# First pair's forward stage and the weight preparation put into the hand-given order, a shorter routing, and a newly searched order

## The chip, the core and the metric

The kernel runs on one core of a Trainium2 chip. The core has five engines with one instruction queue each: TensorE (PE, matmuls; PEld is its weight loading), VectorE (DVE), ScalarE (ACT), GpSimd (POOL) and SyncE (SP, which here only issues transfers). An engine takes its instructions strictly in the order of its queue, so one that waits holds all behind it. Transfers run on 16 DMA engines that all queues share. The metric is the device time of one execution in microseconds (us); lower is better.

## What is computed

The reference is two layers. For x of 8 batches x 1856 rows x 256 columns:

```python
X = rfft(x, axis=1)                       # 929 complex rows per batch
Yr = shrink(Xr @ w_r - Xi @ w_i + b_r)    # shrink(v) = sign(v) * max(|v| - 0.01, 0)
Yi = shrink(Xr @ w_i + Xi @ w_r + b_i)
x  = irfft(Yr + 1j * Yi, n=1856).reshape(14848, 256)
g  = argmax(x @ w_group)                  # 4 groups, then 4 experts of the group
e  = argmax(x @ w_expert[g])
out = softmax weight of g * softmax weight of e * (relu(x @ w1[g, e]) @ w2[g, e])
```

Each of the 14848 rows (tokens) goes through one of 16 experts (256 to 1024 to 256).

## The kernel before, in words

The 8 batches are worked as 4 pairs. For each pair the kernel runs these stages, each a function whose calls are "steps" named by one letter:

- `c` (`a_mm`, 8 per pair): first-stage DFT matmuls of x (L327) into a PSUM bank; `d` (`a_turn`, 16 per pair): VectorE transposes of the bank (L331). There are three such banks (`pa`, `bufs=3`), shared by many steps.
- `e f h i g` (`f_mm` L599 and copies and subtractions that split the result in a high and a low part), then `j y z k m o` (spectral matmuls L642 and L657 against the prepared weights, bias, shrink).
- `r s` (`b_mm` L682, `b_turn` L690), `v w x` (`p_mm` L701, `p_out` L713 with a store to `ys_d` in DRAM, `p_turn` L723): inverse transform.
- `G H` (gate logits), `R` (`route_steps`: one instruction of `route_g` each, 33 per half pair, 264 in all): which expert a token goes to and which slot of that expert's list. `S` (`scatter`, 128 in all): one indirect transfer each, issued by GpSimd, that writes 128 tokens' (row, weight) entries into the lists `lst` in DRAM (L242). From the 65th on at most five are on their way at once.
- Early expert work on the first rows of four experts' lists, 8 jobs: `I` loads a piece of the lists (L779), `Z` turns it into indices on GpSimd, `F` gathers the rows from `ys_d` (L427, GpSimd), `T X Y` transpose and split them (L804), `U A B` multiply by w1 (L825, 12 matmuls a step), `D E J` multiply by w2 (L849 and L851 in turn, 4 of each a step), `K` stores (L507, GpSimd). `W V` split the weights, `l` loads x and weights (SP).
- `L` loads all lists (L882, L886), `M` gathers the first rows of the main loop (`gi_h`).

The string `ORDER` lists the letters. Each letter runs the next step of its kind, and within it TensorE, VectorE, ScalarE, SP and GpSimd keep that order exactly; nothing is moved at run time. Behind `ORDER` comes the main expert loop over all 16 experts, which is fixed.

Two parts stand ahead of the order in the version before: the first pair's first stage (8 x `lead_mm`, each with two `turn_a`), and the preparation of the spectral weights (`wh`, `wl`, `wsum`, `bias`: L363 to L370). There the build's own scheduler sets the order. In `ORDER` of before, `c` and `d` stand for pairs 1 to 3 alone (24 and 48), and two loads (`CI`, `wg`) are held behind the first pair's last transpose (`a_last`).

Of the kernel before, what the change touches and what calls it, by code (L numbers as in the profile page):

```python
# [36 lines left out]
ORDER = """  # L37
jcddjcdedffehhiicggfhyzfydzkimdhokiejmggfocjfhyyzdkzihkmigogjmeffcoyhdjziykhzkedgigcmmojdefyfodhjyhizizkggdmkcoemjfoyjhz
ykifdmdzkghicmogjoyjffdyzkhmhizkidgmoeegjyfofzhjyihkizmggokjmfeyozhkfijhieggmoyfjfyhzzhikiggmkmffojrosjyshhyiirlzkmggssz
rksorsmojsyscejzdffdcdhihyllkgzigdmvcwcxxlwvdodjdkdxwyxzvcmwwcxkdddxvdwcxmwxcwdddooGdvHRexwjRRfwvxRRjfhywRxRzRhRvxiRigww  # L40
kRgmRRxReRxvRowwRxyRfjRhRzRReyiikRwxRRRzgkmRgfRRomoRfjjRlRhhGyiyHRzfRRRgkRSzmkhRRRRSigomRojefjeRyyRlRzhkzfRiRRShRRSSSRRS
SmgRioRgjRkfymRRhiiRzkSggeofmjoRRSSjhRfhyfihiyrgSzgksrzmkRsmssSrSoosjjeyszfhfyrhkizkmgssiSRvomgjoxcdwjwvxdxRSyyzRwzwvxwe
xffSxvkxwShwhwxikmmGoSSiojSjvgSwRSgHRxRRxRRvcwxRydywRdxvRRwcxlzSzRRwwdRvxSRkRRxkRdewmRxwfcoRfRhjRiGShgRSmddSRoiHcRgeyfRd
SjdfhiRzRRhyzRRSklikgmeSgRmoSRfocRRjSjRchfRSdigySRdzRRydSkmzdkeRRhciRSSoSmlRjSgodjRyfzRRRhfydSkRRSRlzRShmReiikojRggRfSyR
mRRRfeRhzRhiSoRikjgSgRymojrzfhSfiyhiszgkSRkgmmsRroojjRyRszSysrsszkmrWSosSSefkjSsvfmhShigSigxWowvwSyxxSvvwwxVxjezwwyfSkwx
fxmzhxhiSSRokmVSwogWiVjWGgvvHvRyxRwjxxRwRvRRRwxSRxRzRwRweSxwfyzRhRRkRxfRwxmkwRhiReRRmgRioRRGfgRjoRSRIhWRRRWWZyjyzRRiiRzk
keggSSHRmfohmojRRfSyjhRzyfRihkRzSRgiRRmRgkmoSRejfoyfRjzhyRSzRRhSSiiSSRgVkSgmRkSojRRyRRmRzSRRkVRRRomSVorRRRRsFWTsRFRXYVSr
sSUsrlURVslsABABrSSSsSSWUAsVUBWvvWAwxwvxBVwxWDVWSxVWSSVxwDEDlvWJSwwwxxSDSwExSVJVTXGYHvWvxwwRvSxRwxxvVRRUwRAwSBRUSAxSIUBZ
wWwlUFRRAFTXRWxxBYRRABWDRFUDKVRRRWUxABEwAVTBRRUDRRWRJAURARRBRRFRRWRRXRFDGBVRRKSSSRYUUSHRARVRRBTlASDVUEBRAVWUBSWDDDXARJVE
ESVRJDYJRWUBASRKUAFBRSRRRDSWUSBKUKSTRRRRKXRRDSADRVEVRARSRWYBRVlBEWRWRJRUARUTAWRSSVDRWKWDRRBBSSUUADVASXBJESSSYDBUUDJABKSA  # L50
TUEBUAVBASVDVXBEYSDSDUUJAJRSSDESSSSBDJAUDKBUDEKKLKAABJBEDJDEMKDDKEJJKK
"""
# [68 lines left out]
def spectral_moe(ctx: ExitStack, tc: tile.TileContext, x, wri, bri, wgate, w1, w2, cst, out):  # L121
# [241 lines left out]
    nc.scalar.copy(out=wc, in_=wraw[:, 1])  # L363
    nc.vector.tensor_tensor(out=wsum, in0=wraw[:, 0], in1=wraw[:, 1], op=ALU.add)
    nc.vector.tensor_tensor(out=wraw[:, 0], in0=wraw[:, 0], in1=wraw[:, 1], op=ALU.subtract)
    for i, w_ in enumerate((wraw[:, 0], wsum)):
        nc.scalar.copy(out=wh[:, i], in_=w_)
        nc.vector.tensor_tensor(out=wl[:, i], in0=w_, in1=wh[:, i].bitcast(F32), op=ALU.subtract)
    nc.vector.tensor_tensor(out=bias[:, D:], in0=bias[:, D:], in1=bias[:, 0:D], op=ALU.subtract)
    nc.scalar.copy(out=sl, in_=craw)  # L370
# [856 lines left out]
```

## Time and profile before

| what | us |
|---|---|
| median of 3 runs | 1098.86 (1097.95 to 1099.74) |
| the profiled execution, its own time | 1100.85 |
| its span, first to last instruction | 1098.9 |
| PE busy | 1055.3 (96%) |
| PEld busy | 872.6 (79%) |
| DVE busy | 692.2 (63%) |
| ACT busy | 512.9 (47%) |
| POOL busy | 391.1 (36%) |
| mean granted TensorE clock | 0.983 of full |

The profile's second part cuts the span in 40 slices of 27.5 us. PE is at 6 tenths in the first, at 9 or more nearly everywhere else, with dips to 7 and 8 in slices that begin near 302, 357 and 440 us. The granted clock is below 9 tenths in the first slice only. DMA is busy at 9 tenths and moves 381 GB/s in the first slice; it is at 2 to 6 tenths in most others.

### The profile page before, as it was taken

Reading aid. Unit: us, or ns where it says so; the run is one execution under the profiler, and the core shown is the slowest. Engines: PE = TensorE matmul, PEld = TensorE weight load, DVE = VectorE, ACT = ScalarE, POOL = GpSimd, SP = SyncE. Lnnn points to the kernel's source line nnn. Section 1 sums busy time; section 2 is a strip of 40 time slices with the busy share of each in tenths; the row PEclk is TensorE's granted clock in tenths of the full one; section 3 lists DMA queues with packets and bytes.
Section 4 is the critical chain, followed back from the end, with each engine's and each line's share of the span. In section 5 each row is a group of like instructions: output and inputs, shape, how many; then the busy total and the mean of one; then the engine's idle time right before and its main releaser. Section 6 shows DMA issues by size and latency. Waiting matters only on the chain. (4 is left out here: it accounts for less than half of the span.)

```text
span 1098.9 us, 23147 instructions
## 1 busy us (share of the span) xinstructions
PE 1055.3 (96%) x8962; PEld 872.6 (79%) x8962; DVE 692.2 (63%) x1586; ACT 512.9 (47%) x1239; POOL 391.1 (36%) x454
## 2 busy tenths in 40 slices
PE   6999999999979899899999999999999999999996
PEld 2786677776846799798989888798888889798785
DVE  5778999999977674466564646364464835545352
ACT  1554554455616352254554645354454734545352
POOL 0000042345572577623424323433433234334311
PEclk8999999999989899899999999999999999999998
DMA  9500702632356331425324345255333463245300
GB/s 381 197 3 29 261 22 71 163 79 83 76 94 189 135 80 27 156 62 174 128 86 148 122 162 184 81 196 190 130 122 120 151 228 125 83 161 201 117 24 21
DMA packets 42514, 139.11 MB, mean 127 GB/s; under 512 B 17462, under 2 KB 19772, under 8 KB 32034
## 3 DMA queue, kind: packets, MB, share of 16 engines
q1 hardware_dynamic: 21602, 89.22, 23.8%
q0 software_dynamic: 15904, 31.48, 9.3%
q10 hardware_dynamic: 4896, 16.91, 4.8%
q8 instruction: 72, 1.18, 0.5%
q14 instruction: 40, 0.33, 0.1%
HBM read 103.49 MB, written 35.00 MB: 126 GB/s over the span
## 5 line engine op out<-in xcount | busy, mean ns | idle before, releaser
L521 PE MATMUL py<-big,hh 128*128 128x512 f32 x824 | 294.1, 398 | 0.0
L460 PE MATMUL ph<-xth,big 128*128 128x384 f32 (+1 forms) x896 | 258.3, 365 | 0.5 <-ACT xth L447 0.5
L522 PE MATMUL py<-big,hl 128*128 128x256 f32 x824 | 230.6, 280 | 0.0
L242 POOL DMA_INDIRECT lst<-ent,sloti x128 | 128.4, 1003 | 251.5 <-DVE xl L621 143.8
L466 DVE SCALAR_TENSOR_TENSOR hl<-ph,hh 128x256 fp32r<-128x256 f32 x448 | 151.2, 379 | 67.8 <-ACT hh L464 65.8
L460 PEld LDWEIGHTS ph<-xth,big 128*128 128x128 f32 x896 | 167.0, 190 | 19.6 <-issue 1.5
L521 PEld LDWEIGHTS py<-big,hh 128*128 128x128 f32 x824 | 154.8, 188 | 34.7 <-issue 3.2
L464 ACT ACTIVATE hh<-ph 128x256 fp32r<-128x256 f32 x448 | 134.2, 352 | 72.7 <-PE ph L460 72.2
L460 PE MATMUL ph<-xtl,big 128*128 128x384 f32 (+1 forms) x448 | 163.4, 365 | 0.0
L507 POOL DMA_INDIRECT out_dram<-yo,si_f x93 | 94.4, 1015 | 177.5 <-DVE yo L529 159.6
L427 POOL DMA_INDIRECT xg<-ys_d,gi_f x93 | 90.5, 973 | 181.8 <-PE pg L443 159.0
L522 PEld LDWEIGHTS py<-big,hl 128*128 128x128 f32 x824 | 155.1, 188 | 0.1
L529 DVE SCALAR_TENSOR_TENSOR yo<-py,ent_f,yo 128x256 f32<-128x256 f32 x93 | 45.0, 483 | 163.9 <-ACT yo L528 163.9
L528 ACT ACTIVATE yo<-py,ent_f 128x256 f32<-128x256 f32 x93 | 44.1, 475 | 190.0 <-PE py L522 190.0
L410 DVE TENSOR_TENSOR big<-xt,big 128x512 fp32r<-128x512 f32 x160 | 108.7, 680 | 0.0
L409 ACT CAST big<-xt 128x512 fp32r<-128x512 f32 x160 | 99.6, 622 | 0.0
L460 PEld LDWEIGHTS ph<-xtl,big 128*128 128x128 f32 x448 | 85.3, 190 | 7.9 <-DVE xtl L448 0.4
L657 PE MATMUL pw<-wh,xh 128*128 128x256 f32 x240 | 67.6, 304 | 2.0 <-DVE pw L647 1.9
L663 ACT ACTIVATE big<-pw,nlam 128x512 f32<-128x512 f32 x60 | 41.3, 690 | 60.1 <-PE pw L657 60.0
L642 PE MATMUL pw<-wc,xd 128*128 128x256 f32 x240 | 61.9, 394 | 1.9 <-ACT pw L636 1.4
L657 PE MATMUL pw<-wl,xh 128*128 128x256 f32 x240 | 62.1, 281 | 0.0
L642 PEld LDWEIGHTS pw<-wc,xd 128*128 128x128 f32 x240 | 42.0, 189 | 20.4 <-ACT pw L636 7.4
(201 smaller groups left out, 1676.9 us busy)
## 6 DMA issues: line engine op xcount, KB each, us to landing
xt<-in_w_dram SPq DMA_DIRECT2D x48, 1024.0 KB, 5.0
ys_d<-ysb ACTq DMA_DIRECT2D x32, 512.0 KB, 4.0
big<-in_w_dram SPq DMA_DIRECT2D x16, 1024.0 KB, 8.2
big<-in_x_dram SPq DMA_DIRECT2D x8, 1024.0 KB, 10.4
xt<-in_x_dram SPq DMA_DIRECT2D x8, 1024.0 KB, 8.5
lst<-ent,sloti POOLq DMA_INDIRECT x128
lst<-zero SPq DMA_DIRECT2D x1, 1920.0 KB, 25.3
xg<-ys_d,gi_f POOLq DMA_INDIRECT x93
```

The source lines that it names most:

```text
L242: ins = nc.gpsimd.indirect_dma_start(out=lst, out_offset=bass.IndirectOffsetOnAxis(ap=sl_, axis=0), in_=en_, in_offset=None, bounds_check= ...
L409: nc.scalar.copy(out=wt[:, 2 * i, cs], in_=raws[i][:, cs])
L410: nc.vector.tensor_tensor(out=wt[:, 2 * i + 1, cs], in0=raws[i][:, cs], in1=wt[:, 2 * i, cs].bitcast(F32), op=ALU.subtract)
L427: ins = nc.gpsimd.indirect_dma_start(out=xg[:, c, :], out_offset=None, in_=ys_d[0:rows, :], in_offset=bass.IndirectOffsetOnAxis(ap=ids.gi[ ...
L460: nc.tensor.matmul(o[:, :n], lhsT=a_[:, ch, fs], rhs=b_[:, ch, 0:n], start=k == 0, stop=k == 5)
L464: nc.scalar.activation(out=hh[:, f, :m], in_=ov, func=AF.Relu)
L466: nc.vector.scalar_tensor_tensor(out=hl[:, f, :m], in0=ov, scalar=0.0, in1=hh[:, f, :m].bitcast(F32), op0=ALU.max, op1=ALU.subtract)
L507: ins = nc.gpsimd.indirect_dma_start(out=out, out_offset=bass.IndirectOffsetOnAxis(ap=ids.si[:, t:t + 1], axis=0), in_=ysb, in_offset=None ...
L521: nc.tensor.matmul(o, lhsT=hh[:, f, ts], rhs=w2b[:, :, f, :], start=f == 0, stop=f == 7, skip_group_check=True)
L522: nc.tensor.matmul(o[:, 0:D], lhsT=hl[:, f, ts], rhs=w2h[:, f, :], start=False, stop=f == 7, skip_group_check=True)
L642: nc.tensor.matmul(y, lhsT=units["xd", pr, k // 2][:, h, k % 2, 0], rhs=wc[:, h], start=False, stop=False, skip_group_check=True)
L657: ins = nc.tensor.matmul(y, lhsT=a_[:, h, k % 2, j], rhs=t[:, j, h], start=False, stop=a_ is xl and h == 1, skip_group_check=True)
```

## The change

Four things are done.

1. The first pair's `c` and `d` become steps of `ORDER` (`pairs` for `later`; 32 and 64 letters), and so does the weight preparation, as 8 steps `Q`. `zys[0]` is taken from its pool at the first `d`. The hold of `CI` and `wg` behind `a_last` is gone.
2. The array `wri` comes in two transfers, and its second half goes straight into `wc`, so that the ScalarE copy of it (L363) goes.
3. `route_g` has 30 steps for 33: the comparison with the maximum and the product with `PRIO` are one instruction (twice), the product with `PM` is merged into the comparison behind it, the addition of the row number moves from VectorE to GpSimd, and `base` is added to 16 elements ahead of the scan and not to 256 behind it.
4. `ORDER` is another string throughout, searched with longer landing times of the transfers.

```diff
-jcddjcdedffehhiicggfhyzfydzkimdhokiejmggfocjfhyyzdkzihkmigogjmeffcoyhdjziykhzkedgigcmmojdefyfodhjyhizizkggdmkcoemjfoyjhz
...
+cccdddcddcddcddcdddddQcddeQQeffhhjfciQgiQghjQdcQQyyzikddfzdkmhgcimojgceofddddcfhjhyyzzdikgimkedogcjmofhideydjzykfzkhimog
...
+        oh = rt.tile([128, 16, 4], F32, name=f"oh_{tag}")[:, 0:n]
+        nc.vector.scalar_tensor_tensor(out=oh, in0=ex, scalar=0.0, in1=kc("PRIO").unsqueeze(1).broadcast_to([128, n, 4]),
+                                       op0=ALU.is_equal, op1=ALU.mult)
+        yield
         nc.scalar.activation(out=ex, in_=ex, func=AF.Exp)
...
-        oh = rt.tile([128, 16, 4], F32, name=f"oh_{tag}")[:, 0:n]
-        nc.vector.tensor_tensor(out=oh, in0=src, in1=mxb, op=ALU.is_equal)
-        yield
-        nc.vector.tensor_tensor(out=oh, in0=oh, in1=kc("PRIO").unsqueeze(1).broadcast_to([128, n, 4]), op=ALU.mult)
-        yield
...
-        nc.vector.tensor_tensor(out=oh, in0=oh, in1=mxb, op=ALU.is_equal)
+        if tag == "g":
+            nc.vector.scalar_tensor_tensor(out=oh, in0=oh, scalar=kc("PM"), in1=mxb, op0=ALU.mult, op1=ALU.is_equal)
+        else:
+            nc.vector.tensor_tensor(out=oh, in0=oh, in1=mxb, op=ALU.is_equal)
...
-        nc.vector.tensor_scalar_add(out=ent[:, :, 0], in0=kc("GID")[:, r0:r0 + n], scalar1=float(pr * PAIR + 1))
-        yield
-        nc.vector.tensor_scalar(out=ohg, in0=ohg, scalar1=kc("PM"), scalar2=None, op0=ALU.mult)
+        nc.gpsimd.tensor_scalar_add(out=ent[:, :, 0], in0=kc("GID")[:, r0:r0 + n], scalar1=float(pr * PAIR + 1))
...
+        firsts = tot.rearrange("p (e r) -> p e r", e=NE)[:, :, 0]
+        nc.vector.tensor_tensor(out=firsts, in0=firsts, in1=base, op=ALU.add)
+        yield
...
-        nc.vector.tensor_tensor(out=v, in0=v, in1=base.unsqueeze(2).broadcast_to([128, NE, n]), op=ALU.add)
-        yield
...
-        nc.vector.tensor_tensor(out=base, in0=base, in1=incf.rearrange("p (e r) -> p e r", e=NE)[:, :, n - 1], op=ALU.add)
+        nc.vector.tensor_copy(out=base, in_=incf.rearrange("p (e r) -> p e r", e=NE)[:, :, n - 1])
...
-    for i in range(8):
-        o = lead_mm(0, i)
-        for bt in range(2):
-            a_last = turn_a(0, i, bt, o[:, bt])
-
...
-    wraw = xp.tile([128, 2, 2, D], F32, name="xt")
-    nc.sync.dma_start(out=wraw.rearrange("p a c e -> p (a c e)"), in_=wri)
+    wraw = xp.tile([128, 2, D], F32, name="xt")
+    wc = cf.tile([128, 2, D], F32, name="wc")
+    for i, t in enumerate((wraw, wc)):
+        nc.sync.dma_start(out=t.rearrange("p c e -> p (c e)"), in_=wri[:, i * 2 * D:i * 2 * D + 2 * D])
...
+    def weight_steps():
+        nc.scalar.copy(out=sl, in_=craw)
+        yield
+        nc.vector.tensor_tensor(out=wsum, in0=wraw, in1=wc, op=ALU.add)
+        yield
+        nc.vector.tensor_tensor(out=wraw, in0=wraw, in1=wc, op=ALU.subtract)
+        yield
+        for i, w_ in enumerate((wraw, wsum)):
+            nc.scalar.copy(out=wh[:, i], in_=w_)
+            yield
+            nc.vector.tensor_tensor(out=wl[:, i], in0=w_, in1=wh[:, i].bitcast(F32), op=ALU.subtract)
+            yield
+        nc.vector.tensor_tensor(out=bias[:, D:], in0=bias[:, D:], in1=bias[:, 0:D], op=ALU.subtract)
+        yield
...
-    late.enter_context(tc.issue_after(a_last.ins))
...
-    @steps_of(later, u8)
+    @steps_of(pairs, u8)
     def a_mm(pr, i):
...
-    @steps_of(later, u8, two)
+    @steps_of(pairs, u8, two)
     def a_turn(pr, i, bt):
```

Three places of the two strings, which the prediction counts in:

| place | before | after |
|---|---|---|
| 13th `r` to first `T` | `rRRRRsFWT` | `rFRRVRssSSFrRRsT` |
| 96th `S` to third `T` | `SIUBZwWwlUFRRAFT` | `SURwIVZWRARAxRRDBEFBwJEJRRFDRFRDKVREKWT` |
| 128th `S` to the end | `SBDJAUDKBUDEKKLKAABJBEDJDEMKDDKEJJKK` | `SDABUUJAEKEBJKJABDULDAKBKDDDEMJKEJDEJKKK` |

## Rows read from the trace of the kernel before

**Rows 1.** Busy time by window: stretch, length, engines' busy us (count), granted clock, DMA share, GB/s.
```profile
33.00:310.40 277.40, 270.65 (x4110) 201.75 (x4108) 245.55 (x542) 140.92 (x307) 79.97 (x85) 1.00 0.32 93
310.40:315.10 4.70, 0.01 (x1) 0.04 (x1) 3.16 (x4) 0.00 (x0) 3.66 (x4) 0.98 0.85 71
315.10:322.00 6.90, 6.79 (x45) 3.29 (x46) 3.01 (x4) 0.59 (x1) 5.19 (x6) 0.52 0.11 31
354.70:360.20 5.50, 0.07 (x2) 0.06 (x1) 1.03 (x2) 0.31 (x1) 3.84 (x6) 0.92 0.77 274
442.90:448.70 5.80, 1.33 (x6) 0.60 (x6) 0.93 (x3) 1.42 (x3) 4.59 (x9) 0.94 0.81 326
455.50:1098.90 643.40, 632.51 (x3550) 550.65 (x3548) 340.05 (x825) 310.73 (x811) 218.78 (x265) 1.00 0.38 130
```

**Rows 2.** What PE waited for between 306 and 460 us: us in total, times, longest.
```profile
PE bank L804 <- DMA xg<-ys_d,gi_b: 5.4, 1, 5.4
PE bank L804 <- DMA xg<-ys_d,gi_a: 4.7, 1, 4.7
```

**Rows 3.** PE at the start, in order of time: start, length, instruction, [idle before, releaser].
```profile
15.10 1.09 PE L327 MATMUL bank<-big,cA 64*64 64x512 f32 x8 [0.15 <-PE bank L327]
23.17 3.69 PE L327 MATMUL bank<-big,cA 64*64 64x512 f32 x16 [6.98 <-DMA big<-in_x_dram]
26.61 2.56 PE L599 MATMUL bank<-T,big 64*64 64x64 f32 x112
...
33.02 0.36 PE L657 MATMUL pw<-wh,xh 128*128 128x256 f32 x1
```

**Rows 4.** VectorE at the start, in order of time.
```profile
8.87 6.08 DVE L331 STREAM_TRANSPOSE big<-bank 128x512 f32<-128x512 f32 x10
17.42 0.69 DVE L364 TENSOR_TENSOR xd<-xt 128x512 f32<-128x512 f32 x1 [2.46 <-DMA xt<-in_wri_dram]
...
22.56 1.30 DVE L331 STREAM_TRANSPOSE big<-bank 128x512 f32<-128x512 f32 x2
```

**Rows 5.** Transposes of `s` and routing by line and shape: busy us, mean ns | idle before.
```profile
L690 DVE STREAM_TRANSPOSE big<-bank 128x1024 f32<-128x1024 f32 x32 | 38.5, 1230 | 6.4 <-PE bank L682 6.3
...
L221 DVE TENSOR_TENSOR t<-t,base 128x256 f32<-128x256 f32 x8 | 3.4, 419 | 0.2
L200 DVE TENSOR_SCALAR oh_g<-oh_g,K 128x64 f32<-128x64 f32 x8 | 2.3, 289 | 0.0
L170 DVE TENSOR_TENSOR oh_g<-L,mx_g 128x64 f32<-128x64 f32 x8 | 1.7, 212 | 0.0
L198 DVE TENSOR_SCALAR ent<-K 128x16 f32<-128x16 f32 x8 | 1.4, 173 | 0.1
L233 DVE TENSOR_TENSOR base<-base,inc 128x16 f32<-128x16 f32 x8 | 1.3, 162 | 0.0
L259 POOL TENSOR_SCALAR ixt<-ixt 128x10 f32<-128x10 f32 x1 | 0.3, 275 | 0.1
```

**Rows 6.** GpSimd: first gather, last scatter ahead of the second list, last scatter of all.
```profile
308.90 1.00 POOL L427 DMA_INDIRECT xg<-ys_d,gi_a  x1 [0.30 <-issue]
...
341.37 0.97 POOL L242 DMA_INDIRECT lst<-ent,sloti  x1 [0.30 <-issue]
...
432.38 0.98 POOL L242 DMA_INDIRECT lst<-ent,sloti  x1 [0.30 <-issue]
```

**Rows 7.** SP: the second list load, its issue, and what it waited for.
```profile
350.95 0.38 SPq L779 DMA_DIRECT2D ent_b<-lst  x1
...
SPq L779 <- DMA lst<-ent,sloti: 13.5, 1, 13.5
```

**Rows 8.** PE inside the early expert work, in order of time.
```profile
421.34 0.28 PE L825 MATMUL ph<-xth,big 128*128 128x256 f32 x1
421.45 0.39 PE L849 MATMUL bank<-big,hh 128*128 128x512 f32 x1
...
421.80 0.40 PE L849 MATMUL bank<-big,hh 128*128 128x512 f32 x1
```

More of the change, by code (lines that the diff above doesn't have):

```diff
@@ L37 @@
 ORDER = """
-jcddjcdedffehhiicggfhyzfydzkimdhokiejmggfocjfhyyzdkzihkmigogjmeffcoyhdjziykhzkedgigcmmojdefyfodhjyhizizkggdmkcoemjfoyjhz
-ykifdmdzkghicmogjoyjffdyzkhmhizkidgmoeegjyfofzhjyihkizmggokjmfeyozhkfijhieggmoyfjfyhzzhikiggmkmffojrosjyshhyiirlzkmggssz
-rksorsmojsyscejzdffdcdhihyllkgzigdmvcwcxxlwvdodjdkdxwyxzvcmwwcxkdddxvdwcxmwxcwdddooGdvHRexwjRRfwvxRRjfhywRxRzRhRvxiRigww
-kRgmRRxReRxvRowwRxyRfjRhRzRReyiikRwxRRRzgkmRgfRRomoRfjjRlRhhGyiyHRzfRRRgkRSzmkhRRRRSigomRojefjeRyyRlRzhkzfRiRRShRRSSSRRS
@@ L42 @@
[L42 to L51, printed above, removed]
+cccdddcddcddcddcdddddQcddeQQeffhhjfciQgiQghjQdcQQyyzikddfzdkmhgcimojgceofddddcfhjhyyzzdikgimkedogcjmofhideydjzykfzkhimog
@@ new lines @@
+gfmjhoiejfcygyzzhkkimmdgoocjyfjfyhzdihzkmikmogegjojyffzyddzkhhkmieeoigmgjfojhfyzykmhzkioiggjemffoyjzhhkiiggemfoyjzhfyzkk
+hiiggrmfohmjlfyojissyzhzrigkgmsrlskoesjmfsrhoysijysfzzcghcddigkvcdmldxwcwxvoddjwkxxdylmdvwwvxzxxcwwkwdxdcocddddGmjvewffo
+HRRyxxRhRhzwRRcidgivRgRdkmRjwvoRjxxeRwyRRwxyRRwzRRRvxkRRRwzRfxmxRkhwRiGogRRRiegmRoHjRySjfhzfSyhRizkfkRSRSgShmiRSRoRRemSj
+SRSgoeRRySfzfhjiyRSRhiRzkRRgmRoRRkRgfhjRmRielyRRgliRzoRgkjfRRmhofSyfhjhiiRzggrRysSzskrmkssrmooejjfSfysshhiRyzzirkmkggssS
+vmowxcojjwdxvwdSyyxvSSzxwzwvexxkwwSxfkfwmmxhoSGhjoigvigRHScwxwSvxjwdRdSRSxcSwyxdRvwdRxeSzvxRlywxzSSwkRffkRhRmRxwRSRoiRhg
@@ new lines @@
+RRiRefgRRGmhfjRcSSRolhjRHyRidyzRRidgRzRgkkmRmRSRcefRcoRRjfddoSRShhjicyygRRSSzSdSidzRdkRkdmmeRgoSjRSofcjRhyylzRdRzkRfRikd
+SgSemhSiSRSRojRgRmRRfyRRRojRfzhkhilRgRiemgRSofRhRjfihgSSiyzryRSSsgkrzkssrmosssmSjyorjezWksSSWsyffmvhihoSzvjwxxikSgwwgSxx
+mwyvowvexjSzwffxxyVSRzWkwSWkhiSVwxhgeimVffGgoWSmhiVShjSoijvggwHvSyyRxxRwRRzxwwRkRRmxRzvlRvowRxxjeRRwRxywRwRRRzkRmfRWRRkx
+mWoRRhiiRRRRogRGjjIgRyRzyWHSfRkRezRhRRSSRmRfoRjkyhfRhmzSSeSiZikoggjfRRhymzkRfojiRySgSRRmhRRizogjRRkSSVyRRRzmoVVSSRSkmRor
+FRRVRssSSFrRRsTXYsrsSUrsWAlsWUWAsBBSSvwxxvSvwxwwvSRVWxxwSVxVxwwUTSwSUxWASDBWXGSWVYHSRAvRvWSlSBSVxwSwUxAUDxDAVVRRwBRxRBRR
@@ L52 @@
+vwSvRRwxUWxxwSURwIVZWRARAxRRDBEFBwJEJRRFDRFRDKVREKWTXDFRRlDRWYUUAABERTVBVFURWRRAURGARBSBXRWYUHVTURSVSRRRASlJRRRASBDRDUBV
+URJXYARSDKERRWSRSTDASESRRDBJBSWVUURWWJRKKARVABSDRWURlEVBAUBASSRVKXDRRDYRRBFRURURAATSBWRBDEJSSVSSUWUVWJVDRDASSXDWBADSSYBS
+UATVBKESSUSAUDSSJWADBBUEASEDVVJKXBSDYUSDABUUJAEKEBJKJABDULDAKBKDDDEMJKEJDEJKKK
 """
@@ L313, in new_z @@
         return big.tile([128, KP // 2, 2, 128, 2], F32, name="big")
-    zys = {0: new_z()}
+    zys = {}
     x_in = {}
@@ L358, in spectral_moe @@
     x1 = load_x(1)
-    wc = cf.tile([128, 2, D], F32, name="wc")
     wh = cf.tile([128, 2, 2, D], F32R, name="wh")
@@ L362, in spectral_moe @@
     wsum = wf.tile([128, 2, 2, 128], F32, name="xd").rearrange("p c q n -> p c (q n)")
[L363 to L370, printed above, removed]
+    def weight_steps():
[12 more added lines that the diff above has]
+        yield
     nlam = cf.tile([128, 1], F32, name="nlam")
@@ L895, in spectral_moe @@
     steps = dict(
-        l=load_steps(), c=a_mm, d=a_turn, e=f_mm, f=f_high, h=f_low, i=d_copy, g=d_sub, j=m_bias, y=m_common, z=m_share, k=m_mm,
+        Q=weight_steps(), l=load_steps(), c=a_mm, d=a_turn, e=f_mm, f=f_high, h=f_low, i=d_copy, g=d_sub, j=m_bias, y=m_common, z=m_share, k=m_mm,
         m=m_relu, o=m_shrink, r=b_mm, s=b_turn,
```

## The prediction

> **What bounds the kernel now.** I read the table of windows first, then what PE waited for, then the start engine by engine. The main loop is one long PE stretch: 632.5 of 643.4 us busy at full clock [rows 1]. The change does not touch it, so only the 455 us ahead of it are at stake. There, from 33 to 310 us, PE is busy 270.7 of 277.4 us and VectorE 245.6 (89%) [rows 1]. The reader should see that PE sets the pace and VectorE is close behind: a VectorE instruction saved here gives nothing directly, a PE gap closed gives its whole length.
>
> The gaps are few. (a) The start: PE ends the first pair's matmuls at 15.10 + 1.09 = 16.2 us, stands 7.0 us until a piece of the second pair's x lands, and starts L599, which needs nothing but the first pair's transposes and T, at 26.61 [rows 3]. (b) 310.4 to 315.1: the first `T` waits 4.7 us for the first gather. (c) 354.7 to 360.2: the third `T` waits 5.4 us for the gather behind the second list [rows 1, 2]. (d) 442.9 to 448.7, ahead of the main loop: PE is busy 1.33 of 5.8 us [rows 1]. Behind (b) the clock is granted at 0.52 for 6.9 us: the lower level, 1.2 GHz, after PE had stood 4.7 us. That costs 6.9 x 0.48 = 3.3 us more [rows 1]. I estimate the same 3.3 behind (c) and (d), whose gaps are as long. So (b) costs 8.0, (c) 8.7, (d) about 8.
>
> **The start.** VectorE does ten transposes in 6.08 us, then stands 2.46 us for the weights, and then mixes five weight instructions of 0.4 to 0.7 us with the last six transposes, which end at 22.56 + 1.30 = 23.9 [rows 4]. In the new string all 16 `d` of the first pair stand ahead of any VectorE `Q`: from 8.87 they take 16 x 0.61 = 9.7, so they end near 18.6 if the banks keep up; I take 18.9. And `e` stands ahead of the second pair's first `c`, so L599 can start at 18.9 and not 26.6. T must have landed by then: it is issued directly ahead of the weights and x of the second pair, and the weights had landed at 17.42 [rows 4].
>
> That is 7.7 us at this point, but most is not kept. From L599 to the first L657 before took 33.02 - 26.61 = 6.4 us [rows 3]; now five weight instructions stand between, 0.69 (L364 [rows 4]) each at most, so 3.1 to 3.5 more. 18.9 + 6.4 + 3.3 = 28.6 against 33.0. Of these 4.4 us one `c` that was done before and now is still to do takes 1.1 (the eight matmuls of 15.10 [rows 3]). The lead is 3.3; I take 3. It can be 0 (if the next `c`, which still needs the x that lands at 23.17, holds all behind it on PE, or the clock stays at 0.52 until PE has worked a while), and up to 6 if the chain of copies is hidden by the second `e`. The split of `wri` in two adds one issue on SP and no bytes; the ScalarE copy L363 that it removes hung on nothing that was late. The loads behind the former hold on `a_last` were issued after the second pair's x anyway, so I put them at nothing; should they slip ahead of it, x would land later by their 1.3 MB, some 3 us at the 381 GB/s of the page's first slice, which takes the lead away (in the 0).
>
> **Routing.** Per half pair on VectorE: two comparisons of 0.21 go into the products beside them, -0.42; the product with PM (0.289) goes, and its scalar comes into a 0.21 comparison, which then costs 0.21 to 0.29, so -0.21 net; the row number (0.173) goes to GpSimd; adding `base` falls from 0.419 to about 0.162, the 16-element sum, though its operand now lies in PSUM (at worst 0.419) [rows 5]. Sum -1.06, eight times -8.5 us, at least -6.4. All of it lies beside PE work in a stretch that PE sets [rows 1], so I cost it at nothing. If that cover were gone, because VectorE sets the pace, up to the whole 8.5 would be gained on top; I leave it out, as rival 2 shows the price of a VectorE that binds. The lower bound is a loss: GpSimd gets eight additions of about 0.28 plus the 0.30 that it spends between instructions [rows 5, 6], 4.6 us in all. No one on VectorE waits for them, only the scatters behind them on GpSimd itself. GpSimd is busy 4.59 of 5.8 us in (d) and issues without a break up to the last scatter [rows 1, 6]; there one of the eight counts, 0.6 us at most. The scan now waits for the addition ahead of it, which needs `base` of the half pair before: that has been ready for tens of us.
>
> **Gap (b).** Before, the gather is issued at 308.90 and its rows are there at 315.1, 6.2 us on, with nothing for PE in between (`F W T`) [rows 1, 6]. Now a whole `r` stands between, with two `s` ahead of it and one behind. As only three banks exist, that `r` waits for two transposes (L690) of 1.23 us [rows 5], and the `T` for one. So PE still loses about 2.5 + 1.2 = 3.7 us here, in two pieces with work between, which may leave the clock up. Where there were 8.0 there are 3.7 to 7.0: I take 3 saved. Bounds: 0 (the gather is issued as much later), 6.
>
> **Gap (c).** The 96th scatter is issued at 341.37, and the load of the list that it fills is issued at 350.95, when the scatter has landed: 8.6 us from its end. SP stood there 13.5 us [rows 6, 7]. From that `S` to the third `T` PE had `U U` to do, now `U D D D`. A `U` is 12 matmuls that start 0.11 apart, a `D` four pairs that start 0.35 apart, so each is 1.4 us [rows 8]: 2.8 before, 5.6 now. The wait falls from 5.4 to about 2.6, and if so short a gap keeps the clock up, 3.3 more is saved: 2.8 to 6.1. I take 4; bounds 0 (the scatter comes that much later in the new order) and 8.7.
>
> The Trainium skill (DMA: Bandwidth & Descriptors, Anatomy of one DMA, SWDGE path) has a transfer issued from GpSimd cost about 2.0 us beyond its bytes. This trace does not agree: 8.6 us, beside large loads. By the page the list would have been loaded at 344.3, and (c) would not exist at all.
>
> **Gap (d).** From the last `S` to the end of the string PE had nine `U` and `D`, now ten: 1.4 us more beside the same chain of list load, `M` and gathers; GpSimd has the same four stores ahead of `M`. Less 0.6 for the additions: 1 saved, bounds -3 and 4.
>
> **Sum.** 3 + 3 + 4 + 1 = 11. A new string will not be as tight over the 277 us as the old one was (6.7 us of PE idle [rows 1]); I take off 1, bounds 0 and 5. That leaves 10. Against the profiled execution (1100.85 us, span 1098.9) this is 1090.9; that run lies 2.0 above the median, so the median falls from 1098.86 to **1089**, with 1083 to 1095 as this case's own range.
>
> **Rivals.**
> 1. *The gaps (b) and (c) close altogether.* If scatters land in about 2 us in the new order because no large load runs beside them, the list load is 6.6 us earlier. That is more than the wait that is left at either place. 8.0 + 8.7 + 3 + 1 - 1 = 20: 1079. For it: DMA is busy at 0.77 right behind that slow landing [rows 1]. Against it: the same loads of weights have to run somewhere near, and banks still hold (b).
> 2. *The lead is given back.* VectorE sets the pace in the middle, and the waits come back at other letters: within 2 us, 1098. For it: 89% on VectorE. Against it: PE is at 98% there, and VectorE has 6 us less to do.
> 3. *Slower: the last 32 scatters become the bound.* They are issued 1.28 us apart; at most five may be on their way, so the rate falls as soon as one takes more than 5 x 1.28 = 6.4 us to land. At the 8.6 us seen ahead of (c), each takes 1.72: 32 x 0.44 = 14 us more on GpSimd, whose last scatter ended just 9.5 us before PE ran out [rows 1, 6], so nearly all of it lengthens (d). Less the 10 saved: +4, 1103. For it: the limit exists and such a landing was seen once. Against it: the last scatter of all waited for no other, only the 0.30 of issue [rows 6].
>
> **How the numbers follow.** Forecast 0.61, rival 1 0.14, rival 2 0.14, rival 3 0.11. The range reaches into rival 1 to 1081 and over rival 2 to 1099. A run of this kernel tells 0.2% (2.2 us) from no change. Faster by more: 0.61 + 0.14 + 0.05 of rival 2 = 0.80; within: 0.07; slower: 0.02 of rival 2 + 0.11 = 0.13.
>
> **What would show it.** L599 first starts near 19 us and the first L657 near 29 to 30; the wait of PE for `gi_a` is gone or under 2 us and that for `gi_b` under 3; the windows behind them show a granted clock near 1; the gaps ahead of the main loop end near 439 and not 448.7; the routing's VectorE time falls by 6 to 9 us. The forecast is wrong if the first L657 comes at 32 or later, if new waits of PE of more than 5 us in sum stand between 33 and 310 us, or if scatters wait for scatters behind 380 us.

## The result, and the profile after

The median falls from 1098.72 us (1097.95 to 1099.74, 4 runs) to 1087.16 us (1085.40 to 1088.37, 4 runs): ratio 0.9893 [0.9876, 0.991]. The forecast was 1089 from a median of 1098.86. A second series of the same kernel (`after_again`, below) gave 1087.29, ratio 0.9922 [0.9897, 0.9947]. The profiled execution took 1086.77 us, 14.1 less than the one before. In time it is the predicted case; the sum behind it is not: between the two profiles the start and gap (c) gave twice what I took for them, gap (b) half, and to undo the shorter routing, put at nothing, costs time in the new string.

The page of the kernel after, its first part:

```profile
span 1085.0 us, 23145 instructions
...
PE 1052.1 (97%) x8962; PEld 871.2 (80%) x8962; DVE 685.8 (63%) x1554; ACT 512.1 (47%) x1238; POOL 397.8 (37%) x462
```

VectorE's time falls by 6.4 us, in 32 fewer instructions; PE does the same matmuls. Windows of the kernel after (columns as in [rows 1]): the stretch up to the last `o`, gap (b) and what follows it, the place of gap (c), gap (d) and what follows it, and the rest.

```profile
28.20:302.60 274.40, 267.20 (x4086) 202.28 (x4084) 241.56 (x520) 141.41 (x307) 78.83 (x87) 1.00 0.33 101
302.60:310.30 7.70, 4.75 (x64) 1.48 (x65) 6.24 (x9) 0.00 (x0) 6.17 (x6) 0.98 0.53 171
310.30:317.00 6.70, 6.70 (x38) 2.34 (x39) 2.17 (x3) 0.59 (x1) 4.95 (x5) 0.51 0.40 42
349.00:361.00 12.00, 12.00 (x87) 10.88 (x85) 7.08 (x18) 6.17 (x14) 8.45 (x10) 1.00 0.73 246
429.30:435.70 6.40, 2.29 (x11) 1.04 (x9) 0.85 (x3) 1.33 (x3) 5.29 (x10) 0.78 0.83 334
435.70:442.00 6.30, 6.21 (x24) 5.81 (x25) 2.95 (x13) 1.66 (x6) 4.91 (x6) 0.68 0.25 79
442.00:1085.00 643.00, 632.06 (x3548) 550.23 (x3546) 340.07 (x825) 310.66 (x810) 220.28 (x266) 0.99 0.37 130
```

The kernel before, behind its gaps (c) and (d):

```profile
360.20:367.00 6.80, 6.80 (x29) 6.33 (x30) 3.66 (x10) 3.48 (x7) 5.28 (x6) 0.57 0.38 111
448.70:455.50 6.80, 6.79 (x22) 6.43 (x23) 2.77 (x12) 1.49 (x6) 5.28 (x6) 0.55 0.26 78
```

(Its page shows the clock at 8 tenths in the slices near 302, 357 and 440 us and in the last one too, not in the first alone as the section on its profile says.)

Read against [rows 1]: gap (c) is gone (PE busy 12.00 of 12.00 at full clock). Gap (b) is in part filled with work, yet the clock behind it is at 0.51, its lower level, as it was before. Gap (d) stands. What PE waited for from 302 to 460 us, beside [rows 2]:

```profile
PE pg L447 <- DMA xg<-ys_d,gi_h: 3.6, 2, 2.9
PE bank L808 <- DMA xg<-ys_d,gi_a: 2.4, 1, 2.4
PE bank L686 <- DVE big L672: 1.5, 1, 1.5
PE bank L738 <- DVE yt L727: 1.1, 1, 1.1
PE bank L705 <- DVE big L694: 0.9, 1, 0.9
PE bank L686 <- DVE big L694: 0.6, 1, 0.6
```

There is no wait for `gi_b` any more. Of the four short waits for VectorE three are new; the kernel before had the one of `r` for the last `o` (here L686 for L672) as well, with 1.3 us. PE at the start, beside [rows 3] (L603 is the former L599, L661 the former L657):

```profile
15.29 1.09 PE L328 MATMUL bank<-big,cA 64*64 64x512 f32 x8 [0.15 <-PE bank L328]
16.44 0.34 PE L603 MATMUL bank<-T,big 64*64 64x64 f32 x4
18.19 0.35 PE L603 MATMUL bank<-T,big 64*64 64x64 f32 x8 [1.41 <-DVE big L332]
18.79 2.67 PE L603 MATMUL bank<-T,big 64*64 64x64 f32 x116 [0.25 <-DVE big L332]
22.62 3.98 PE L328 MATMUL bank<-big,cA 64*64 64x512 f32 x16 [1.17 <-DMA big<-in_x_dram]
...
28.25 0.45 PE L661 MATMUL pw<-wh,xh 128*128 128x256 f32 x1
```

The stand of 7.0 us for x is down to 1.2, and L661 starts 4.8 us sooner. Where PE stood at the same steps, read from each profile (us, start of the first or last matmul of a kind, for `k` of `wh` with `xh`; main loop: its first matmul):

| kernel | first `k` | first `r` | last `k` | last `v` | last `D` | main loop | span |
|---|---|---|---|---|---|---|---|
| before | 33.0 | 89.1 | 306.3 | 348.3 | 442.3 | 448.7 | 1098.9 |
| after | 28.2 | 82.9 | 300.5 | 345.6 | 429.3 | 435.7 | 1085.0 |
| after_again | 26.2 | 80.9 | 297.4 | 341.8 | 425.5 | 433.5 | 1083.7 |
| start_alone | 28.9 | 82.4 | 298.4 | 337.2 | 431.2 | 439.8 | 1088.7 |
| no_start | 32.1 | 86.8 | 303.4 | 348.2 | 431.9 | 438.6 | 1087.6 |
| route_alone | 33.0 | 88.5 | 310.2 | 349.1 | 446.2 | 452.5 | 1103.4 |
| route_placed | 32.8 | 88.6 | 306.9 | 343.9 | 438.0 | 443.7 | 1094.4 |
| route33 | 27.3 | 82.1 | 305.6 | 350.4 | 434.4 | 439.6 | 1089.5 |
| gid_vector | 28.0 | 82.8 | 301.2 | 343.8 | 435.1 | 440.5 | 1089.3 |

After against before: 5.8 us at the last `k`, 13.0 at the last `D`, 13.0 at the main loop, 13.9 at the end.

### The profile page after: what moved, and what is told of

It reads as the page before. It is cut to its first block, busy times and chain, and to the rows that moved or that the text cites. A ratio compares the mean times of both kernels' runs of the same rounds, so it can differ in the third digit from the quotient of the medians.

```text
span 1085.0 us, 23145 instructions
## 1 busy us (share of the span) xinstructions
PE 1052.1 (97%) x8962; PEld 871.2 (80%) x8962; DVE 685.8 (63%) x1554; ACT 512.1 (47%) x1238; POOL 397.8 (37%) x462
## 5 line engine op out<-in xcount | busy, mean ns | idle before, releaser
L243 POOL DMA_INDIRECT lst<-ent,sloti x128 | 130.6, 1020 | 233.2 <-DVE xl L625 130.0
L661 PE MATMUL pw<-wh,xh 128*128 128x256 f32 x240 | 68.1, 306 | 2.7 <-DVE pw L651 2.7
L661 PE MATMUL pw<-wl,xh 128*128 128x256 f32 x240 | 62.1, 281 | 0.0
L646 PEld LDWEIGHTS pw<-wc,xd 128*128 128x128 f32 x240 | 42.2, 189 | 18.5 <-issue 4.4
## 6 DMA issues: line engine op xcount, KB each, us to landing
big<-in_x_dram SPq DMA_DIRECT2D x8, 1024.0 KB, 11.6
```

Source lines behind the costliest of these rows:

```text
L243: ins = nc.gpsimd.indirect_dma_start(out=lst, out_offset=bass.IndirectOffsetOnAxis(ap=sl_, axis=0), in_=en_, in_offset=None, bounds_check= ...
L646: nc.tensor.matmul(y, lhsT=units["xd", pr, k // 2][:, h, k % 2, 0], rhs=wc[:, h], start=False, stop=False, skip_group_check=True)
L661: ins = nc.tensor.matmul(y, lhsT=a_[:, h, k % 2, j], rhs=t[:, j, h], start=False, stop=a_ is xl and h == 1, skip_group_check=True)
```

## The experiments

Each comparison is with the kernel before on the same chip in the same series (its medians there: 1096.7 to 1097.6 us).

**The start alone, and all but the start.**

```diff
# start_alone: before, with parts 1 and 2 of the change
-jcddjcdedffehhiicgg...
+cccdddcddcddcddcdddddQcddeQQQQQQQjcddjcddffehhiicgg...
# no_start: after, without parts 1 and 2: the first 8 c, 16 d and all Q out of the string
```

> The kernel before with the start of the changed kernel alone: the first pair's c and d and the Q stand ahead of its old string, one e is moved to the front, routing and the rest of the string stay. Theory A (PE sets the pace, so a lead won at the start is kept): L599 first at 18 to 19 us as in the changed kernel, the first L657 near 28 to 30 us and not 33, and the time falls by 3 to 6 us, to 1093 to 1096. The rival (VectorE sets the pace in the middle and the lead is given back): the first L657 is early too, but the time stays within 2 us of before, 1097 to 1100.

> The changed kernel with its start undone: the first pair's c, d and all Q are taken out of the new string and stand ahead of it as in the kernel before, with wri in one transfer. Theory A: the start is worth 5 to 6 us (first L657 28.25 against 33.02 us, first L682 82.9 against 89.1), so 1092 to 1093.5 and the gain of the rest of the string, some 6 us against before, stays. The rival (the lead is given back, the gain lies all in the later gaps): 1087 to 1089.5.

Measured: start_alone 1090.12 us, 0.9939 [0.9925, 0.9954]; no_start 1091.45 us, 0.9953 [0.994, 0.9966]. start_alone gained more than theory A's 3 to 6 us, and no_start lies between the two forecasts, nearer to theory A. The lead is kept: in the old string it is 6.7 us at the first `r` and still 7.9 at the last `k`; taken out of the new string, 3.9 are lost at the first `r` and 2.9 at the last `k`. The start is worth 3 to 7 us, the least by no_start against the second series of the kernel after, whose intervals touch; I took 3.

**The routing alone, and all but the routing.**

```diff
# route_alone: before, with part 3; per half pair the letters R at places 5, 15, 28 of 33 out (from 0)
# route_placed: the same, two pairs of steps share one letter; places 4, 5, 14, 15, 22, 28 out
-        yield
         oh = rt.tile(...)          # behind the subtraction
...
-        yield
         incf = rt.tile(...)        # behind the sum of firsts and base
# route33: after, with the routing of before; R doubled at places 4, 13, 19 of 30
```

> The kernel before with the 30-step routing alone: three R of each half pair are taken out of the old string, nothing else is moved. Theory A (PE sets the pace, the 1 us of VectorE per half pair is hidden): within 2 us of before, 1097 to 1101. The rival (VectorE sets the pace): 4 to 8 us are gained, 1091 to 1095.

> The changed kernel with the old 33-step routing: three R of each half pair doubled in the new string, the row number added on VectorE again. Theory A (hidden under PE): within 2 us of the changed kernel, 1086 to 1089.5. The rival (VectorE sets the pace): 4 to 8 us lost, 1091 to 1095.

> The kernel before with the shorter routing alone, as in route_alone, but placed otherwise: the fused instruction shares a letter with the subtraction ahead of it, the sum of firsts and base shares one with the scan, and six letters R per half pair are taken from the string (old places 4, 5, 14, 15, 22 and 28 of 33), so that the exponential, the matmuls, the scan and everything behind stand in the very letters they had before. Theory 'misplaced': route_alone was 5 us slower only because its exponential, its sum and its matmuls came a letter later or earlier; here the time is that of the kernel before or up to 5 us less (1092 to 1098, ratio 0.995 to 1.000), VectorE's wait for the exponential and for the firsts is that of before. Rival 'the new instructions themselves' (the add on GpSimd ahead of scatters, the add into PSUM ahead of the scan): 3 us or more slower than before again (ratio 1.003 or more), with the last k of the fourth pair at 309 us or later (before: 306.3).

Measured: route_alone 1102.66 us, 1.0046 [1.0032, 1.006]; route33 1091.28 us, 0.9946 [0.9933, 0.9959]; route_placed 1099.48 us, 1.0023 [1.0009, 1.0037].

Neither theory of route_alone had a loss of more than 2 us, and route_placed lies between its two. So 32 VectorE instructions less made the old string slower: by 5 us with operations that stood a letter off, by 2 with most in their former letters. What PE waited for in route_alone, 80 to 320 us, where before had 1.9 us of the first kind and 1.3 of the second:

```profile
PE pw L658 <- DVE pw L648: 3.5, 7, 0.7
...
PE bank L683 <- DVE big L669: 2.1, 1, 2.1
```

In the new string the 33 steps cost time. Windows of 82 to 300 us of the kernel after, and then of route33:

```profile
82.00:300.00 218.00, 212.84 (x3229) 156.03 (x3228) 198.56 (x436) 112.13 (x243) 76.84 (x85) 1.00 0.34 104
```

```profile
82.00:300.00 218.00, 210.46 (x3197) 152.56 (x3197) 198.75 (x442) 110.16 (x238) 70.79 (x76) 1.00 0.34 104
```

VectorE is equally busy in both, 91%, and PE gets 2.4 us less done in route33. Five profiles of this string with 30 steps (after, after_again, t3_early, plus, gid_vector) have PE at 212.3 to 213.4 us in this window and the last `k` at 297.4 to 301.2; route33 has 210.5 and 305.6, outside both. In time it is 2.6 to 5.8 us behind (0.9946 against 0.9922 and 0.9893; its interval overlaps that of the second series). This is not a full VectorE: in the same window it was busy 201.6 us in the kernel before and 203.5 in start_alone, with PE at 215.6 and 213.7. Which of the added instructions hold PE is not shown. In route_placed, theory "misplaced" accounts for about half of the loss; its last `k` (306.9) is 0.6 us behind before, its profiled execution was the fastest of twelve (1096.28 to 1104.51), and where the median loses the other 2 us is not settled.

**Which of the instructions taken from VectorE count** (32 in all, four per half pair).

```diff
-        nc.gpsimd.tensor_scalar_add(out=ent[:, :, 0], ...)
+        nc.vector.tensor_scalar_add(out=ent[:, :, 0], ...)
```

> The kernel after, with one instruction of each routing (the add of the row number, eight in all) back on VectorE in place of GpSimd. Theory 'VectorE's time counts in the new string': eight instructions of about 0.23 us with their gaps come back, of 24 that the shorter routing took from VectorE; route33 lost 4 to 5 us with all of them, so 1 to 2 us more than the kernel after (ratio 0.990 to 0.992). Rival 'only the instructions on the chain to PE count' (the exponential, the matmuls' inputs; the row number is needed by the scatters alone): within 0.7 us of the kernel after (ratio 0.9885 to 0.9905).

Measured: 1087.86 us (1081.31 to 1091.11), 0.9904 [0.988, 0.9928]: the ratio lies in both forecasts and its interval covers both, so the run does not decide between them; the last `k` is 0.7 us later. But its profile shows a wait of 4.9 us for `gi_b`, which the kernel after does not have, and that led on to gap (c).

**Gap (c): cover, or landing.**

```diff
# t3_early: after, third T X Y right behind the third F
-BEFBwJEJRRFDRFRDKVREKWTXDFRRlDRWYUUA
+BEFTXYBwJEJRRFDRFRDKVREKWDFRRlDRWUUA
# load_later: before, 13th l behind the second I; 17th W where the 18th stood, 18th behind the third Y
-DEDlvWJS...SxSIUBZwWwlUFRRAFTXRWxxBYRRA
+DEDvWJS...SxSIlUBZwwlUFRRAFTXRWxxBYWRRA
# load_latest: before, both l further back, with the W and V that need them
-DEDlvWJS...SxSIUBZwWwlUFRRAFTXRWxxBYRRABWDRFUDK...
+DEDvWJS...SxSIUBZwwUFRRAFTXRxxBYlRRABDRFUDK...
```

> The kernel after, with one change in the string: the third T, X and Y (transposes of the first rows of the second list) stand right behind the third F instead of five letters of PE work later, so the cover that gap (c) got is taken away. Theory 'scatter landed sooner': in the kernel after, the rows of the third F lay there about 3.1 us before T came (about 349.9 against 353.04), since the 96th scatter landed 3.9 us after its issue instead of 8.6 us; with about 2.8 us of cover gone, a wait for gi_b of 0 to 1 us appears and the time stays within 1.5 us of the kernel after (1086 to 1089, ratio to before 0.988 to 0.992). Rival 'the cover did it' (the prediction's own step: 2.8 us of PE work more ahead of the third T): the wait that the kernel before had comes back with 2.5 to 5.4 us, and the time is 2.5 to 5 us longer than the kernel after (1090 to 1092, ratio 0.992 to 0.994).

> The kernel before, with one change in the string: the 1 MB expert weight load that SP issued at 337.06, just ahead of the 96th scatter's landing, stands behind the second list load, and the conversion that needs it (17th W) behind the third Y. Theory 'the load beside the scatters': the 96th scatter lands in about 4 us as in the kernel after (before: 8.6 us), SP's wait for it falls from 13.5 us to 4 to 9, PE's wait for gi_b from 5.4 us to under 2, and the time falls by 3 to 6 us (1092 to 1095, ratio 0.994 to 0.997). Rival 'the place of the scatters, or the cover': the 96th scatter still lands 8 us or more after its issue (other transfers beside it: the stores of transformed rows), the wait for gi_b stays at 4.5 to 6 us, and the time is within 1.5 us of before (ratio 0.9985 to 1.0015).

> The kernel before, with the two 1 MB expert loads around the second list (issued at 337.06 and 354.54 there) moved behind the third Y and 27 letters further, and the conversions that need them behind those. In load_later, where both loads were issued together at 347.2, the 96th scatter landed in 2.5 us instead of 8.6, but the third gathers beside the loads took 7.6 us instead of 4.4, and nothing was won. Theory 'whatever lies beside the 1 MB loads lands late': here the scatter lands in 2 to 4 us and the gathers in 4 to 5 us, the third T stands 5 us or more earlier than before (360.2 there), PE's wait for gi_b is 0 to 3 us, and the time is 2 to 5 us less than before (1092 to 1095.5, ratio 0.9955 to 0.998). Rival 'the loads only trade places with something else' (stores of transformed rows, conversions that come late): gi_b wait of 4 us or more, or new waits for the conversions as large as what is won; the time within 1 us of before (ratio 0.999 to 1.001) or more.

Measured: t3_early 1089.70 us, 0.9922 [0.9906, 0.9939]; load_later 1096.76 us, 0.9994 [0.9983, 1.0006]; load_latest 1097.30 us, 1.0001 [0.9989, 1.0013].

In t3_early the cover is gone and no wait for `gi_b` returns (third `T` at 350.33, 4.4 us behind its second gather). But in this profile PE came to that `T` 18.7 us behind the 96th scatter, in the kernel after 19.2 with 2.8 us of cover more: the scatter went out 2.3 us earlier against PE's work. So the run shows that the gap can stay closed without the cover, not that the cover had no part. Its time lies between the two forecasts and does not tell it from the kernel after.

load_later shows what lies beside the landings. GpSimd's 96th scatter, SP's list load and the expert loads, and the third `T`, which waits for its two gathers in turn:

```profile
338.98 0.97 POOL L242 DMA_INDIRECT lst<-ent,sloti  x1 [0.31 <-issue]
...
349.57 0.95 POOL L427 DMA_INDIRECT xg<-ys_d,gi_b  x1 [0.31 <-issue]
```

```profile
342.42 0.38 SPq L779 DMA_DIRECT2D ent_b<-lst  x1
...
347.22 2.94 SPq L571 DMA_DIRECT2D xt<-in_w_dram  x2
```

```profile
353.93 0.66 PE L804 MATMUL bank<-K,xg 128*128 128x128 f32 x2 [3.43 <-DMA xg<-ys_d,gi_b]
357.23 0.69 PE L804 MATMUL bank<-K,xg 128*128 128x128 f32 x2 [2.64 <-DMA xg<-ys_d,gi_b]
```

With the load gone from beside it (the last one went out at 319.23), the scatter lands 342.42 - 339.95 = 2.5 us after its end; it took 8.6 in the kernel before [rows 6, 7], where the second load went out at 337.06. load_latest, with no load there either, has 3.3. But both loads now run beside the gathers: the second takes 357.2 - 349.6 = 7.7 us, where the kernel before took under 3 (357.24 to 360.17), and PE waits 6.1 us in two pieces. The wait moved; nothing was won. In load_latest the first load went out at 348.92 all the same, 0.1 us behind the second gather: the letter of an `l` fixes its place among SP's own issues alone; this one stood 3.5 us for ScalarE's `ysb` (a store that it is held behind) and then went out. That run could test its theory for the scatter alone.

**The kernel after again, a splice, and two repairs.**

```diff
# splice: start_alone's string up to the sixth half pair's routing (33 steps), then after's (30)
# plus: after, one S from ahead of the first F to behind it; three K to behind the 128th S and M
-SRSkmRmorFRRV...KXBSDYUSDABUUJAEKEBJKJABDULDAKBKDDDEMJKE
+SRkmRorFSRRV...XBSDYUSKDABUUJAEKEBJKJABDULDABDDDEMKKJKE
```

> Two strings joined: up to the sixth half pair's routing the string of start_alone (its start, then the order of the kernel before, routing in 33 steps there), behind it the string of the kernel after, with routing in 30 steps for the fourth pair. start_alone had its last k at 298.4 us and its last r at 316.2, the kernel after 300.5 and 319.6; behind that the kernel after had no wait for gi_b and start_alone one of 5.5 us. Theory 'the parts add': the last k at 298 to 299, no wait for gi_b, 1083 to 1086 us (ratio to before 0.986 to 0.989), 1 to 3 us better than the kernel after. Rival 'the two parts aren't independent' (scatters reach the join in another state, so their landings move): the 96th scatter lands 6 us or more after its issue, a wait for gi_b of 2 us or more, 1087 to 1091 us.

> The kernel after, with two edits that its trace points to. First, the scatter in front of the first F stands behind it, so that the first gathers go out about 1 us earlier (303.6 in the kernel after; the pool they write opens at 302.6), and the wait for gi_a falls from 2.4 to about 1.4 us. Second, a row store between the last scatters stands behind the 128th, and two more behind M, so that the last list and the gathers behind it come about 2 us earlier (the list's load 421.95, the gathers 426.2 there), and the wait for gi_h falls from 3.6 to 1.5 to 2 us. Theory 'landings set both gaps': 2 to 3 us less than the kernel after (1083.5 to 1085.5, ratio 0.986 to 0.988). Rival 'the clock and the stores decide': at half clock PE has the work behind gap (b) to do anyway, and the delayed row stores hold the output buffers, so ScalarE waits and with it the main loop: no change within 1 us, or up to 3 us more (ratio 0.989 to 0.993).

> The kernel after, unchanged, profiled and timed once more. In seven kernels that share its late string or most of it, PE's wait for gi_b was 0 in four profiled executions (the kernel after, no_start, route33, t3_early) and 4.3 to 4.9 us in three (splice, gid_vector, plus); the 96th scatter's landing went with it. Theory 'the landing differs from execution to execution': times spread over 4 us or more (1084 to 1091), the median is 1087 to 1089, above the 1087.2 of the first four runs, and the profile may show either case (no wait with the 96th scatter's list load 5.5 us or less behind its issue, or a wait of 3 to 5 us with 6 us or more). Rival 'the string of the kernel after fixes it': times within 3 us of each other around 1086 to 1087.5, no wait for gi_b, the list's load 4 to 5.3 us behind the 96th scatter's issue as in the first profile (4.85).

Measured: splice 1092.42 us (1086.47 to 1096.36), 0.9941 [0.9915, 0.9968]; plus 1089.60 us, 0.9928 [0.9914, 0.9942]; after_again 1087.29 us (1084.29 to 1091.31). None beats the kernel after. splice is slower than both of its forecasts, plus is in its rival's range, and after_again spreads over 7 us, as its theory had it. In plus both small steps did about what was expected of them, and a third wait took more than they gave:

```profile
PE bank L808 <- DMA xg<-ys_d,gi_b: 4.3, 1, 4.3
...
PE pg L447 <- DMA xg<-ys_d,gi_h: 1.6, 2, 0.8
PE bank L808 <- DMA xg<-ys_d,gi_a: 1.6, 1, 1.6
```

The eight kernels with the late part of the new string either have the wait for `gi_b` or not. Issue times of the third `F`'s second gather (GpSimd) and of the 1 MB expert load nearest to it (SP), with PE's wait for `gi_b`, from their profiles:

| kernel | gather | load | gather ahead by | wait |
|---|---|---|---|---|
| t3_early | 345.91 | 352.07 | 6.2 | 0 |
| route33 | 350.96 | 355.65 | 4.7 | 0 |
| after | 347.00 | 350.66 | 3.7 | 0 |
| after_again | 343.94 | 346.83 | 2.9 | 0 |
| no_start | 351.35 | 353.50 | 2.2 | 0 |
| plus | 349.63 | 349.87 | 0.2 | 4.3 |
| splice | 349.40 | 349.47 | 0.1 | 4.9 |
| gid_vector | 349.04 | 348.84 | -0.2 | 4.9 |

The rows of gid_vector: GpSimd, SP, and PE at the two halves of the third `T`.

```profile
335.01 0.97 POOL L243 DMA_INDIRECT lst<-ent,sloti  x1 [2.64 <-DMA lst<-ent,sloti]
...
349.04 0.96 POOL L431 DMA_INDIRECT xg<-ys_d,gi_b  x1 [0.31 <-issue]
```

```profile
341.89 0.38 SPq L783 DMA_DIRECT2D ent_b<-lst  x1
...
348.84 0.33 SPq L575 DMA_DIRECT2D xt<-in_w_dram  x1
```

```profile
351.18 0.38 PE L808 MATMUL bank<-K,xg 128*128 128x128 f32 x2
356.46 0.69 PE L808 MATMUL bank<-K,xg 128*128 128x128 f32 x2 [4.90 <-DMA xg<-ys_d,gi_b]
```

The same rows of the kernel after, with the load beside its 96th scatter and the landings of its gathers:

```profile
333.83 0.98 POOL L243 DMA_INDIRECT lst<-ent,sloti  x1 [0.30 <-issue]
...
347.00 0.96 POOL L431 DMA_INDIRECT xg<-ys_d,gi_b  x1 [0.31 <-issue]
```

```profile
335.04 0.33 SPq L575 DMA_DIRECT2D xt<-in_w_dram  x1
338.68 0.38 SPq L783 DMA_DIRECT2D ent_b<-lst  x1
...
350.66 0.33 SPq L575 DMA_DIRECT2D xt<-in_w_dram  x1
```

```profile
353.04 0.60 PE L808 MATMUL bank<-K,xg 128*128 128x128 f32 x4
```

```profile
DMA to landing us min/median/max: 4.4/4.9/5.3
```

And those of the kernel before:

```profile
334.99 0.97 POOL L242 DMA_INDIRECT lst<-ent,sloti  x1 [5.38 <-DMA lst<-ent,sloti]
...
357.24 0.95 POOL L427 DMA_INDIRECT xg<-ys_d,gi_b  x1 [0.31 <-issue]
```

```profile
323.40 13.99 SPq L571 DMA_DIRECT2D xt<-in_w_dram  x2
...
354.54 0.33 SPq L571 DMA_DIRECT2D xt<-in_w_dram  x1
```

```profile
360.17 1.09 PE L804 MATMUL bank<-K,xg 128*128 128x128 f32 x4 [5.43 <-DMA xg<-ys_d,gi_b]
```

In gid_vector as in the kernel after, the first gather is ahead of the load, and its half of `T` starts in time. The second lands 7.4 us on when it goes out with the load (356.46 - 349.04); that of the kernel after took 5.3, the longest of those shown. This does not make the load the cause: a store of transformed rows goes out with it (350.66 and 350.67 in the kernel after), and in the kernel before a load went out 2.7 us ahead of the second gather, which landed in under 3.

Two things tell the profiles apart: how far the 96th scatter runs ahead of PE, and how long the chain behind it takes. Us by which, from 296 to 350 us, scatters waited for scatters; then, counted from the issue of the 96th, when PE came to the third `T` and when the second gather's rows were there; and the wait for `gi_b`:

| kernel | 96th scatter | scatters waited | PE at third `T` | rows there | wait |
|---|---|---|---|---|---|
| before | 341.37 | 6.0 | 13.4 | 18.8 | 5.4 |
| load_later | 338.98 | 4.8 | 11.5 | 18.2 | 6.1 |
| splice | 334.57 | 5.3 | 17.2 | 22.5 | 4.9 |
| plus | 336.17 | 3.3 | 16.1 | 20.8 | 4.3 |
| gid_vector | 335.01 | 2.9 | 16.2 | 21.4 | 4.9 |
| after_again | 330.92 | 2.0 | 18.3 | 17.8 | 0 |
| no_start | 336.48 | 1.5 | 19.1 | 17.7 | 0 |
| t3_early | 331.64 | 0.5 | 18.7 | by 18.7 | 0 |
| after | 333.83 | 0.3 | 19.2 | 18.5 | 0 |
| route33 | 337.20 | 0 | 20.6 | by 20.6 | 0 |

The other four profiles fit in: scatters waited 3.8 to 8.4 us, and the wait for `gi_b` is 4.5 to 7.4. From the 96th scatter to the rows the kernel after is no faster than the kernel before, 18.5 us against 18.8: the scatter lands 3.9 us after its end and not 8.6, but list and gathers take 4.4 longer. PE comes to `T` 5.8 us later behind the scatter. Of these, 2.8 are the cover that the prediction counted; by the other 3.0 the scatter is further ahead of PE's work. In all fourteen profiles little waiting of scatters for scatters (0 to 2.0 us) goes with no wait for `gi_b`, and 2.9 us or more with one. No run changed this alone, so it is not shown to be the cause, and why they wait in one and not in another is open. That both happen between executions of one kernel too is likely from the spread of the times (after_again 1084.29 to 1091.31) and was not seen: both profiles of the kernel after lie on the good side.

## Why the prediction was right, and where it was not

- **Start** (3 taken, bounds 0 to 6). The places were right: L599 at 18.9 (18.79 for the bulk), L657 at 28.6 (28.25), VectorE's transposes of the first pair ended at 18.74 (18.6 to 18.9). The term was too small: the 1.1 us taken off for the open `c` was not lost, and at the first `r` the lead is 6.2 us.
- **Routing** (VectorE -8.5, at least -6.4; nothing for the time). VectorE fell by 6.4. The fused comparisons cost 0.216 and 0.284 us, the addition in PSUM 0.177, the one on GpSimd 0.337 (I had 0.28). "All of it lies beside PE work" is the step that failed: in the new string the 33 steps cost 2.6 to 5.8 us (route33), and in the old one the 30 steps cost 2 to 5 (route_alone, route_placed). I had named a gain of up to 8.5 us if the cover were gone and left it out; a loss I had not named. So it hangs on the string; which of the instructions decide is open.
- **Tightness of the new string** (-1). Behind 302 us it lost 1.1 + 0.9 in new waits at `G` and `v`; ahead of 300 us the lead shrank from 6.2 to 5.8. About right, but what the shorter routing gave is hidden in it.
- **Gap (b)** (+3). I had worked out 3.7 us of idle time, for banks. PE stood 2.4 us for the gather at `T` and 0.6 for a transpose at `r`, 2.9 in all with the hundredths; its 1.5 for the last `o` is no part of it, as the kernel before had 1.3 there. That this "may leave the clock up" failed in this profile: 6.7 us at 0.51 cost 3.3. So 8.0 became 6.2, and less the 0.2 at the `o` it gave 1.6. The price of 8.0 was high, too (last section).
- **Gap (c)** (+4). It gave 5.4 us of wait and 6.8 us at 0.57, worth 2.9: 8.3. The cover of 5.6 us instead of 2.8 is there, but half of the step was missing: PE came 5.8 us later to `T` behind the scatter, 3.0 of them because the scatter ran further ahead of PE, which goes with 6.0 us of scatters waiting for scatters before and 0.3 now. I had read the landing of the 96th, and not the wait of 5.38 us ahead of the one at 334.99. Rival 1 (0.14) had the price of (c), not that of (b); its condition, no large load beside the scatters, was not met: one went out 0.2 us behind the end of the 96th (335.04).
- **Gap (d)** (+1). The way to the main loop gave nothing (13.0 before and behind it), the clock behind it 0.9: 0.68 now, 0.55 then. The number is right by luck: the tenth step and the additions on GpSimd, from which it was added up, show no gain.
- The sum by these: 5.8 + 1.6 + 8.3 - 2.0 + 0.9 = 14.6, where the span fell by 13.9; the 0.7 between them is not found. Two to four of them belong to the profile of before, which was 1100.85 where its medians were 1096.7 to 1098.9. That 10 was forecast and the median fell by 11.6 is luck in part: errors of +2.8 and +4.3 in the terms stand against -1.4 and -1, and the gaps were read from a profile 2.0 to 4.2 us above the medians.

By the figure of the Trainium skill (DMA: Bandwidth & Descriptors, Anatomy of one DMA, SWDGE path), about 2.0 us beyond the bytes for a transfer issued from GpSimd, the list could follow some 2 us behind the scatter. load_later's 2.5 us is near that, the 3.9 of the kernel after and before's 8.6 are not: of these three the figure fits the scatter with no large load issued near it.

Rival 3 was not seen where I had put it, at the last 32 scatters: behind 350 us no wait of a scatter for a scatter is over 0.3 us, before or after. Its mechanism had been at work in the kernel before all the same, ahead of gap (c).

## What to carry to other kernels

When a wait for a small transfer closes or opens, time its whole chain from the first link, and time when the waiting engine arrives: here one link became 4.7 us shorter and others 4.4 longer, and the wait closed because the chain began earlier against PE's work. A large transfer moved away from one link can land on the next (load_later). An engine that is busy 90% beside a bound one need not be cover: compare what the bound engine gets done in a fixed window before you put its instructions at nothing. A single profile of a string with such races shows one side of them; several kernels that share the string show both.

## What the hardware showed that I had not expected

Gap (b) was not the same in two executions whose string is the same up to there, nor was the clock behind it. In the kernel before PE stood 4.7 us for `gi_a` [rows 2], and the clock then was granted at 0.52 [rows 1]; in load_later PE stood 2.8, and it was 1.00:

```profile
PE bank L804 <- DMA xg<-ys_d,gi_a: 2.8, 1, 2.8
```

```profile
313.30:320.00 6.70, 6.70 (x84) 3.58 (x85) 5.21 (x9) 1.18 (x2) 5.18 (x6) 1.00 0.12 26
```

In the five other profiles with this order around the gap PE stood 2.3 to 3.1 us, with 0.75 or 1.00 behind it; start_alone, 3.1 us:

```profile
305.60:312.50 6.90, 6.89 (x72) 3.57 (x80) 4.51 (x7) 1.18 (x2) 5.13 (x6) 0.75 0.07 14
```

So some 2 us of this gap's wait and up to 3.3 us behind it were one execution's, and the 8.0 of the prediction was at the high end. The length of the wait does not settle the clock: in the new string it was 0.51 behind 2.4 us in the kernel after, 0.75 behind 2.3 in after_again and 1.00 behind 1.8 in gid_vector.
